# Windowed attention and a gated FFN: one planner for all engines, 32-query units, q and k in 1 KB runs, V as 16 strips, x turned by transfers

## The chip, the cores and the metric

The kernel runs on one core of a Trainium2 chip. The core has a matrix engine (PE, with its weight loads shown as PEld), a vector engine (DVE), a scalar engine (ACT), GpSimd (POOL) and a sync engine (SP), each with its own instruction stream in order; 16 DMA engines move data. POOL and SP issue the transfers here. The metric is device time in microseconds of one execution.

## The reference

Eight batches, eight heads, 512 local and 32 global tokens, head width 64. A global query sees all 544 keys; a local query sees the 32 global keys and the local keys at most 32 positions away. The softmax subtracts the row's maximum. The result, 4352 rows of 512, goes through two products with a gate between.

```python
k_all = concat([k_g, k_l]); v_all = concat([v_g, v_l])
out_g = sm(scale * q_g @ k_all.T) @ v_all
s_ll  = where(abs(pos_q - pos_k) <= 32, scale * q_l @ k_l.T, -1e9)
s_lg  = scale * q_l @ k_g.T
out_l = sm(concat([s_lg, s_ll])) @ concat([v_g, v_l])
x = concat([out_g, out_l]) as (4352, 512)
h = x @ w_in                          # 512 -> 2048
out = (h * clip(h + 3, 0, 6) / 6) @ w_out
```

## The kernel before

All arithmetic on PE is in fp16 with fp32 sums; the loads from POOL's queue convert fp32 to fp16.

**Loads.** `qk_loads` (L98) brings q and k of a batch as four tiles each of 128 tokens, in runs of one head's 64 values (256 bytes in memory). `v_loads` (L110) brings V into `ve`, with the 32 global rows ahead of the local ones, and `shift` (L114, L115) makes `vo`, the same shifted by 64 rows, by two transfers on SP. `load_w_in` and `load_w_out` follow the first batch's loads on POOL.

**Attention.** `pair_qk` (L180, L183) turns two heads of q and of k by eight transposes of 128x128 into one PSUM tile, and ACT copies it to `qk`. A block is (batch, 128 queries `j`, four heads `qd`), so there are eight local blocks a batch and two global ones. `local_scores` (L202) multiplies units of 64 queries with 128 local and 32 global key columns; four 64x64 parts of the array work side by side. Four times DVE adds the mask, scales and takes the maximum (L210) and ACT takes the exponential (L213). `local_turn` (L221, L223) turns the weights by five transposes; DVE first gathers the global columns of the four heads (`exg`, L215). `local_av_global` (L231) multiplies the global columns with a block-diagonal V (`vgb`, L119); `local_av` (L241) adds the local part with `ve` and `vo`; `normalise` (L255, L256) divides. `local_x` (L264, L268) turns x by four transposes and a DVE copy. `global_scores`, `global_turn` and `global_av` (L283 to L310) do the global queries for four even or odd heads at a time.

**FFN.** `first` (L332) makes 128 columns of h for all 512 tokens of a batch (batch 0 in two halves of 256) by four matmuls into one of three PSUM tiles; ACT (L335) and DVE (L336) make the gate. `second` (L346) sums 16 matmuls for 128 tokens, a quarter at a time; DVE copies (L350), SP stores. The global tokens of all batches come last.

**Order.** Only PE's order is written by hand: per block the value product two blocks back, the scores of this block, the turn of the block before, and between them `fill`, which puts in FFN pieces at a share of 0.8 each time. The other engines get theirs from the framework's scheduler. Transfers use eight completion counters on each of POOL's and SP's sides, and a buffer's load waits for its last readers.

## Time and profile before

| | |
|---|---|
| median of three runs | 411.99 us (411.43 to 412.63) |
| span of the profiled execution | 409.9 us |
| granted PE clock | 1.00 |
| packets of the DMA engines, share of POOL's queue | 117874, 58.7% |

The profiled execution's own time is its span and what lies around it; the three runs stand about 2 us above the span. The page gives per engine the busy time, its share and the instruction count; the slices are fortieths of the span in tenths of busy time. In the groups a line reads: line, engine, operation, output and inputs with sizes, count, then busy time, mean nanoseconds of one, and the idle time before them with what ended it. The stage table lists a stretch, its length, PE's busy time and count, the granted clock, the DMA engines' busy share (packets of one engine overlap, so it can pass 1.00), and GB/s. Matmuls overlap, so the time that one costs is the distance to the start of the next.

### The profile page before, as it was taken

The page shows a single profiled execution, that of the slowest core. Times are in us where ns is not written, and L with a number is a line of the kernel's source. Part 1 is how long each engine was busy: PE and PEld are TensorE (multiplying, and loading weights), DVE is VectorE, ACT ScalarE, POOL GpSimd, SP SyncE. Part 2 cuts the span into 40 slices and gives each one's busy share as a digit, 9 for nine tenths or more (in the row PEclk, how much of TensorE's full clock was granted, in tenths as well). Part 3 has the DMA queues.
Part 4 walks back from the last instruction along what each step waited for, and adds up shares of the span by engine and source line. Part 5 has one row for each costly group of instructions (what it writes and reads, how often), then busy time and mean ns, then how long its engine had stood idle before and what let it go on. Part 6 is the DMA issues. An engine that isn't in the chain of part 4 may idle for free.

```text
span 409.9 us, 10488 instructions
## 1 busy us (share of the span) xinstructions
PE 358.8 (88%) x4104; PEld 201.7 (49%) x4104; DVE 265.1 (65%) x1073; ACT 253.3 (62%) x549; POOL 120.0 (29%) x166
## 2 busy tenths in 40 slices
PE   0516388799999999999999999999999999999996
PEld 0404256565545554555445545554555455444642
DVE  2414357885689568865896669756984698558611
ACT  1624368885678658965786668756976586446500
POOL 8925996920920074006500370004000000000000
PEclk9999999999999999999999999999999999999999
DMA  9999999941990199107920493019201100110021
GB/s 90 87 219 200 160 145 126 159 35 53 115 152 3 43 100 137 41 28 91 150 55 27 68 165 60 26 40 92 57 19 36 54 2 2 53 54 0 2 77 77
DMA packets 117874, 31.75 MB, mean 77 GB/s; under 512 B 109888, under 2 KB 111936, under 8 KB 117824
## 3 DMA queue, kind: packets, MB, share of 16 engines
q0 software_dynamic: 111552, 17.84, 58.7%
q1 hardware_dynamic: 6272, 13.24, 9.9%
q8 instruction: 32, 0.52, 0.5%
q14 instruction: 18, 0.15, 0.1%
HBM read 35.65 MB, written 8.91 MB: 109 GB/s over the span
## 4 chain that ended last, share of the span: by engine, by line
PE 58%; DVE 15%; ACT 11%; POOL 7%; DMA 5%; issue 3%; ACTq 0%; POOLq 0%
PE m L346 29%; PE m L332 12%; DVE gt L336 8%; ACT ex L213 6%; DMA win<-in_moe_w_in_dram 4%; ACT t L335 3%; PE t L180 3%; PE t L221 3%; PE a L241 3%; DVE sm L210 3%; PE s L202 3%; ACT et L226 2%; PE a L231 2%; POOL qn L98 2%; POOL kn L98 2%
## 5 line engine op out<-in xcount | busy, mean ns | idle before, releaser
L332 PE MATMUL m<-xt,win 128*128 128x512 f16 (+1 forms) x576 | 122.3, 358 | 7.1 <-DVE gt L336 5.7
L346 PE MATMUL m<-wout,gt 128*128 128x512 f16 x512 | 121.6, 379 | 0.0
L213 ACT ACTIVATE ex<-sm,mx 128x160 f16<-128x160 f32 x256 | 89.0, 418 | 47.2 <-DVE mx L210 47.2
L336 DVE SCALAR_TENSOR_TENSOR gt<-t,m 128x512 f16<-128x512 f32 (+1 forms) x144 | 84.2, 623 | 21.1 <-ACT t L335 20.7
L335 ACT ACTIVATE t<-m 128x512 f32<-128x512 f32 (+1 forms) x160 | 77.2, 527 | 19.9 <-PE m L332 18.8
L332 PEld LDWEIGHTS <-win 128*128 128x128 f16 x640 | 61.1, 98 | 57.1 <-issue 11.7
L210 DVE CUSTOM_DVE_ANT_0 sm<-s,mask 128x160 f32<-128x160 f32 x256 | 67.7, 319 | 10.2 <-PE s L202 10.0
L346 PEld LDWEIGHTS <-gt 128*128 128x128 f16 x512 | 47.3, 98 | 44.6
L226 ACT COPY et<-t 128x640 f16<-128x640 f16 x64 | 43.9, 686 | 29.9 <-PE t L223 29.9
L350 DVE COPY ot<-m 128x512 f32<-128x512 f32 x34 | 23.5, 691 | 36.8 <-PE m L346 36.8
L183 ACT COPY qk<-t 128x1024 f16<-128x1024 f16 x32 | 32.0, 1007 | 16.9 <-PE t L180 16.9
L98 POOL DMA_DIRECT2D qn<-in_q_l_dram x32 | 29.3, 917 | 36.6 <-PE t L180 35.7
L110 POOL DMA_DIRECT2D ve<-in_v_l_dram x40 | 32.3, 861 | 0.0
L98 POOL DMA_DIRECT2D kn<-in_k_l_dram x32 | 29.4, 920 | 0.0
L241 PE MATMUL a<-vo,et 128*64 128x65 f16 x256 | 20.7, 204 | 9.4 <-DMA vo<-ve 9.4
L180 PE MATMUL t<-ident,qn 128*128 128x128 f16 x128 | 14.2, 232 | 16.0 <-POOL ident masks.py:199 9.6
L256 DVE TENSOR_TENSOR x<-a,rec 128x256 f16<-128x256 f32 x64 | 27.0, 422 | 1.4
L110 POOL DMA_DIRECT2D vgn<-in_v_g_dram x8 | 6.0, 752 | 73.1 <-DVE vgb L119 73.1
L231 PE MATMUL a<-vgb,et 128*128 128x264 f16 x64 | 18.3, 285 | 10.1 <-ACT et L226 7.0
L221 PE MATMUL t<-ident,ex 128*128 128x128 f16 x256 | 26.7, 230 | 0.0
L215 DVE COPY exg<-ex 128x128 f16<-128x128 f16 x64 | 15.9, 249 | 15.3 <-ACT ex L213 15.0
L202 PEld LDWEIGHTS <-qk 64*64 64x64 f16 x1024 | 15.9, 111 | 18.4 <-issue 14.1
(68 smaller groups left out, 378.2 us busy)
## 6 DMA issues: line engine op xcount, KB each, us to landing
out_dram<-ot SPq DMA_DIRECT2D x32, 256.0 KB, 2.0
vo<-ve SPq DMA_DIRECT2D x16, 264.0 KB, 3.8
qn<-in_q_l_dram POOLq DMA_DIRECT2D x32, 128.0 KB, 5.0
kn<-in_k_l_dram POOLq DMA_DIRECT2D x32, 128.0 KB, 5.2
ve<-in_v_l_dram POOLq DMA_DIRECT2D x24, 128.0 KB, 5.2
win<-in_moe_w_in_dram POOLq DMA_DIRECT2D x4, 512.0 KB, 11.6
wout<-in_moe_w_out_dram POOLq DMA_DIRECT2D x16, 128.0 KB, 4.9
ve<-in_v_l_dram POOLq DMA_DIRECT2D x8, 96.0 KB, 5.0
```

The costliest lines, as they stand in the source:

```text
L98: return [lambda o=o, i=i: nc.gpsimd.dma_start(out=o, in_=i) for o, i in work]
L110: work = [lambda o=o, i=i: nc.gpsimd.dma_start(out=o, in_=i) for o, i in work]
L183: nc.scalar.copy(out=dst, in_=ps.rearrange("d (i s) -> d i s", i=2))
L210: nc.vector.tensor_tensor_reduce(out=sm, in0=ps[:, e, pi * U:(pi + 1) * U], in1=m, scale=-scale, scalar=3.0e38, op0=ALU.add, op1=ALU.min, ...
L213: nc.scalar.activation(out=ex[:, h, :], in_=sm, func=EXP, scale=-1.0, bias=mx)
L221: nc.tensor.matmul(out=ps[:, h * P:(h + 1) * P], lhsT=ex[:, h, Sg:U], rhs=ident, is_transpose=True)
L226: nc.scalar.copy(out=et, in_=ps)
L241: nc.tensor.matmul(out=ps[s * HW:(s + 1) * HW, h, 0:D + 1], lhsT=et[:, h * P + s * HW:h * P + (s + 1) * HW], rhs=v[:, j, 4 * qd + h, 0:D + 1],
L332: nc.tensor.matmul(out=ps[:, 0:n], lhsT=w_in_t[m][:, c * P:(c + 1) * P], rhs=x[:, m, 0:n], start=(m == 0), stop=(m == NP - 1))
L335: nc.scalar.activation(out=t1[:, 0:n], in_=ps[:, 0:n], func=RELU, bias=0.5, scale=1.0 / 6.0)
L336: nc.vector.scalar_tensor_tensor(out=g[:, 0:n], in0=t1[:, 0:n], scalar=1.0, in1=ps[:, 0:n], op0=ALU.min, op1=ALU.mult)
L346: nc.tensor.matmul(out=ps, lhsT=gs[c][:, t0:t0 + P], rhs=w_out_t[c], start=(c == 0), stop=(c == NDFF - 1))
```

## The change

The kernel is written anew in its attention and its order; the FFN's arithmetic stays.

- Queries go in units of 32: each unit has 96 local key columns and 32 global ones, 128 in all, on 64x32 parts of the array (`scores` in `local`). A step is (batch, 128 queries) with all eight heads, 32 steps in all; the weights of one head are a 128x128 tile and are turned by one transpose each.
- V stands as 16 strips a batch: `vs` holds for each 32-query unit its 96 local and the 32 global rows on 128 partitions, so one matmul a unit and head makes the whole value product (128x32 parts). Strips of batches 0 and 1 are copied by DVE or POOL, 34 copies each; those of the others go by six transfers on SP, and the global rows by four more in every batch.
- q and k are loaded with four successive tokens on one partition, a run of 1 KB; two loads a batch (eight in batch 0). The transposes make 64 rows each, two heads into one tile (128x64 parts), and the copy to `qkT` undoes the order of tokens.
- x is turned by a transposing transfer on SP, 128x512 each (`to_x`), and the global x likewise.
- Every piece of work is an `Op` with a cost and dependencies; `Plan.run` simulates the five engines and the two transfer queues and emits the instructions of all five in the order found. `pick` chooses on PE: full-array attention work first, work on parts of the array when five FFN pieces have passed, when no FFN piece is ready, or when the array is already divided, else FFN. The plan has no term for the completion counters.
- Masks and identity are made ahead of the first load on POOL; w_in is loaded in halves, and batch 1's q and k come between w_in and w_out.
- The global x goes into the FFN's first product per batch column; buffers: three PSUM tiles for the FFN as before, two banks for scores, one tile for turns, two banks for value products.

The core of the diff, the removed parts first:

```diff
-        def shift():
-            nc.sync.dma_start(out=vo[r][0:HW, :, :, :], in_=ve[r][HW:P, 0:NJ, :, :])
-            nc.sync.dma_start(out=vo[r][HW:P, :, :, :], in_=ve[r][0:HW, 1:NJ + 1, :, :])
...
-    def pair_qk(b, p):
-        st = state[b]
-        ps = t_tile(2 * Sl)
-        for i, nat in enumerate((st["qn"], st["kn"])):
-            for j in range(NJ):
-                c0 = i * Sl + j * P
-                nc.tensor.matmul(out=ps[:, c0:c0 + P], lhsT=nat[:, j, p * P:(p + 1) * P],
-                                 rhs=ident, is_transpose=True)
-        dst = qk[b % 2][p].rearrange("d (i c) -> d i c", i=2)[:, :, Sg:Sg + Sl]
-        nc.scalar.copy(out=dst, in_=ps.rearrange("d (i s) -> d i s", i=2))
...
-            for w, (c0, n) in enumerate(((0, Sg), (Sg, P))):
-                for s in range(2):
-                    for e in range(2):
-                        rows = slice(e * D, (e + 1) * D)
-                        lhs = t[rows, Sg + j * P + s * HW:Sg + j * P + (s + 1) * HW]
-                        if w == 0:
-                            rhs = st["gt"][rows, p, gc:gc + Sg]
-                        else:
-                            k0 = KC + (2 * j + s) * HW
-                            rhs = t[rows, k0:k0 + P]
-                        nc.tensor.matmul(out=ps[s * HW:(s + 1) * HW, e, pi * U + c0:pi * U + c0 + n],
-                                         lhsT=lhs, rhs=rhs)
...
-    def local_x(b, j, x):
-        st = state[b]
-        flat = x.rearrange("q h d -> q (h d)")
-        ps = t_tile(NP * P)
-        for p in range(NP):
-            nc.tensor.matmul(out=ps[:, p * P:(p + 1) * P], lhsT=flat[:, p * P:(p + 1) * P], rhs=ident,
-                             is_transpose=True)
-        if j == 0:
-            st["xt"] = xtp.tile([P, NP, Sl], FP16, tag="xt", name="xt")
-        nc.vector.tensor_copy(out=st["xt"][:, :, j * P:(j + 1) * P],
-                              in_=ps.rearrange("d (p q) -> d p q", p=NP))
...
-        share = 0.8
...
+    SWITCH = 95.0
+    LAT = {"PE": 230.0, "ACT": 160.0, "DVE": 120.0, "POOL": 150.0, "SP": 0.0}
...
+        def begin(op, e):
+            nonlocal count
+            cost = op.cost[op.engine.index(e)] if isinstance(op.engine, tuple) else op.cost
+            if e == "PE":
+                if op.mode != self.pe_mode:
+                    cost += self.SWITCH
+                self.pe_mode = op.mode
+            for r in op.take:
+                self.free[r] -= 1
+            op.start, op.on = self.now, e
+            if isinstance(cost, tuple):
+                issue, moved = cost
+                self.busy[e] = self.now + issue
+                drain()
+                queues[e].append([op, moved, self.now + issue])
+                op.done = math.inf
+                look()
+            else:
+                self.busy[e] = self.now + cost
+                self.work[e] += cost
+                op.done = self.now + cost + op.lat
...
+                    can = [op for op in self.ready[e] if able(op)]
+                    if not can:
+                        continue
+                    op = pick(self, can) if e == "PE" else min(can, key=lambda o: (o.rank, o.at))
+                    if op is not None:
+                        begin(op, e)
+                        moved = True
...
+    def dma(rows, run, issue=None):
+        return (300 + 0.56 * rows if issue is None else issue, rows * (22.6 + run / 27.0) / 16)
+    def moved(rows, run):
+        return (420.0, rows * (22.6 + run / 27.0) / 16)
+    DMA_LAT = 1500.0
...
+    def act(n, ptr=False):
+        return (186.0 if ptr else 50.0) + n / 1.2
+    def dve(n, fast=1):
+        return 65.0 + n / 0.96 / fast
...
+    def loads(b):
+        r = b % 2
+        k = 0
+        prev = [turned[b - 2][p] if b >= 2 else None for p in range(NP)]
+        if b == 0:
+            for p in range(NP):
+                for i, (t, src) in enumerate(((qn, q_l), (kn, k_l))):
+                    hs = slice(2 * p, 2 * p + 2)
+                    nat[b][i][p] = load(t[r][:, hs, :], src[b, hs].rearrange("h (p r) d -> p h (r d)", r=R),
+                                        2 * P, 1024, [], (b, 0, p, i), f"{'qk'[i]}n{b}.{p}")
+        else:
+            for i, (t, src) in enumerate(((qn, q_l), (kn, k_l))):
+                o = load(t[r], src[b].rearrange("h (p r) d -> p h (r d)", r=R), H * P, 1024, prev, (b, 0, i) if b > 1 else (0, 4, 2, i),
+                         f"{'qk'[i]}n{b}")
+                for p in range(NP):
+                    nat[b][i][p] = o
...
+        vdep = [strips[b - 2][i] for i in range(len(strips[b - 2]))] + [av_op[b - 2][NJ]] if b >= 2 else [z[r]]
+        ops = [load(vn[r][0:Sg, NJ, :, 0:D], v_g[b].rearrange("h s d -> s h d"), H * Sg, 256, vdep, (b, 2, 0),
+                    f"vg{b}")]
+        for i in range(NJ):
+            ops.append(load(vn[r][:, i, :, 0:D], v_l[b, :, i * P:(i + 1) * P, :].rearrange("h s d -> s h d"),
+                            H * P, 256, vdep, (b, 2, i + 1), f"vn{b}.{i}"))
+        vload[b] = ops
+        parts = [
+            (flat[W:P], nf[0:Sg, NJ:NJ + 1, :].unsqueeze(2), Sg * NU, [ops[0]], True),
+            (flat[0:W, :, 1, :], nf[0:W, 0:NJ, :], W * NJ, ops[1:], False),
+            (flat[0:W, :, 2, :], nf[Sg:P, 0:NJ, :], W * NJ, ops[1:], False),
+            (flat[0:2 * Sg, :, 3, :], nf[2 * Sg:P, 0:NJ, :], 2 * Sg * NJ, ops[1:], False),
+            (flat[2 * Sg:W, 0:NJ - 1, 3, :], nf[0:Sg, 1:NJ, :], Sg * (NJ - 1), ops[1:], False),
+            (flat[0:Sg, 1:NJ, 0, :], nf[3 * Sg:P, 0:NJ - 1, :], Sg * (NJ - 1), ops[1:], False),
+            (flat[Sg:W, :, 0, :], nf[0:2 * Sg, 0:NJ, :], 2 * Sg * NJ, ops[1:], False),
+        ]
+        free = [av_op[b - 2][j] for j in range(NJ)] if b >= 2 else [z[r]]
+        strips[b] = []
+        if b in MOVED:
+            quads = ((1, 0, W, 0, 0), (2, 0, Sg, Sg, 0), (2, Sg, Sg, 2 * Sg, 0), (2, 2 * Sg, Sg, W, 0),
+                     (3, 0, 2 * Sg, 2 * Sg, 0), (0, Sg, Sg, 0, 0), (0, 2 * Sg, Sg, Sg, 0), (0, 0, Sg, W, -1),
+                     (3, 2 * Sg, Sg, 0, 1))
+            for j in range(NJ):
+                for u, d0, rows, s0, d in quads:
+                    if not 0 <= j + d < NJ:
+                        continue
+                    n = H * D1
+                    o = add(("DVE", "POOL"), (dve(n, 2), 200 + n), None, [ops[j + 1 + d]] + free, (b, 1, j, 9),
+                            lat=150.0, what=f"move{b}.{j}")
+                    def emit(o=o, j=j, u=u, d0=d0, rows=rows, s0=s0, d=d):
+                        eng = nc.vector if o.on == "DVE" else nc.gpsimd
+                        eng.tensor_copy(out=flat[d0:d0 + rows, j, u, :], in_=nf[s0:s0 + rows, j + d, :])
+                    o.emit = emit
+                    strip_j[b][j].append(o)
+                    strips[b].append(o)
+            parts = parts[:1]
...
+    def turn_qk(b, p):
+        r = b % 2
+        def emit():
+            for i, t in enumerate((qn[r], kn[r])):
+                for a in range(R):
+                    c0 = i * Sl + a * P
+                    for e in range(2):
+                        nc.tensor.matmul(out=pst[e * D:(e + 1) * D, c0:c0 + P],
+                                         lhsT=t[:, 2 * p + e, a * D:(a + 1) * D], rhs=ident, is_transpose=True)
+        deps = [nat[b][0][p], nat[b][1][p], idop]
+        dst = qkT[r][p]
+        free = [s_op[b - 2][j] for j in range(NJ + 2)] if b >= 2 else [z[r]]
+        pe = add("PE", 450.0, emit, deps + free, (b, 0, p), mode="128x64", take=("t",), what=f"T{b}.{p}")
+        def emit_copy(i):
+            c0 = i * (Sl + Sg)
+            d = dst[:, c0:c0 + Sl].rearrange("d (p r) -> d r p", r=R)
+            s = pst[:, i * Sl:(i + 1) * Sl].rearrange("d (r p) -> d r p", r=R)
+            return d, s
+        halves = []
+        for i in range(2):
+            halves.append(copy(lambda i=i: emit_copy(i)[0], lambda i=i: emit_copy(i)[1], Sl,
+                               [pe] + halves, (b, 0, p, i), give=("t",) if i else (), what=f"Tc{b}.{p}"))
+        turned[b][p] = halves[1]
...
+    def local(b, j):
+        r, n = b % 2, step[0]
+        step[0] += 1
+        gt = gT[(b // 2) % 2]
+        gc = (b % 2) * 2 * Sg + Sg
+        def scores():
+            for p in range(NP):
+                t = qkT[r][p]
+                for w in range(2):
+                    for u in range(UJ):
+                        c = j * P + u * Sg
+                        for e in range(2):
+                            rows = slice(e * D, (e + 1) * D)
+                            o = pss[u * Sg:(u + 1) * Sg, e, p * P:(p + 1) * P]
+                            if w == 0:
+                                nc.tensor.matmul(out=o[:, 0:W], lhsT=t[rows, c:c + Sg],
+                                                 rhs=t[rows, Sl + c:Sl + c + W])
+                            else:
+                                nc.tensor.matmul(out=o[:, W:P], lhsT=t[rows, c:c + Sg], rhs=gt[rows, p, gc:gc + Sg])
...
+        def turn():
+            for h in range(H):
+                nc.tensor.matmul(out=pst[:, h * P:(h + 1) * P], lhsT=ex[ie][:, h, :], rhs=ident, is_transpose=True)
+        k = n % NET
+        tn = add("PE", 8 * 56.0, turn, exps + [et_use.get(k)], (b, 1, j), take=("t",), what=f"E{b}.{j}")
+        ex_use[ie] = tn
+        tc_ = copy(lambda: et[k], lambda: pst, H * P, [tn], (b, 1, j, 9), fast=2, give=("t",),
+                   what=f"Ec{b}.{j}")
+        def av():
+            for h in range(H):
+                for u in range(UJ):
+                    q = slice(u * Sg, (u + 1) * Sg)
+                    c0 = (h % 4) * D1
+                    nc.tensor.matmul(out=psa[q, h // 4, c0:c0 + D + 1],
+                                     lhsT=et[k][:, h * P + u * Sg:h * P + (u + 1) * Sg],
+                                     rhs=vs[r][:, j * UJ + u, h, 0:D + 1])
+        a = add("PE", 8 * 32.0, av, [tc_] + strip_j[b][j], (b, 1, j), mode="128x32", take=("a",), what=f"A{b}.{j}")
+        et_use[k] = a
+        av_op[b][j] = a
+        ix = n % 3
+        def norm():
+            acc = psa[:, :, 0:4 * D1].rearrange("q c (h d) -> q c h d", d=D1)
+            rr = rec[ix].rearrange("q (c h) -> q c h", c=2).unsqueeze(3)
+            nc.vector.reciprocal(out=rr, in_=acc[:, :, :, D:D + 1])
+            nc.vector.tensor_tensor(out=xs[ix].rearrange("q (c h d) -> q c h d", c=2, d=D), in0=acc[:, :, :, 0:D],
+                                    in1=rr.to_broadcast([P, 2, 4, D]), op=ALU.mult)
+        nm = add("DVE", 120 + dve(H * D), norm, [a, x_use.get(ix)], (b, 1, j, 10), give=("a",), what=f"norm{b}.{j}")
+        def to_x():
+            nc.sync.dma_start_transpose(out=xt[b % 3][:, :, j * P:(j + 1) * P], in_=xs[ix])
+        free = m1_done[b - 3] if b >= 3 else []
+        xo = add("SP", (900.0, 1100.0), to_x, [nm] + free, (b, 1, j, 11), DMA_LAT, what=f"X{b}.{j}")
+        x_use[ix] = xo
+        x_op[b][j] = xo
...
+    state = {"since": 0}
+    PACE = 5
+    def pick(plan, can):
+        att = [o for o in can if o.what[0] in "TEGSA"]
+        ffn = [o for o in can if o.what[0] == "M"]
+        full = [o for o in att if o.mode == "full"]
+        if full:
+            return min(full, key=lambda o: (o.rank, o.at))
+        tiled = [o for o in att if o.mode != "full"]
+        if tiled and (not ffn or state["since"] >= PACE or plan.pe_mode != "full"):
+            same = [o for o in tiled if o.mode == plan.pe_mode]
+            order = {"128x64": 0, "64x32": 1, "128x32": 2}
+            o = min(same or tiled, key=lambda o: (order[o.mode], o.rank, o.at))
+            if plan.pe_mode == "full":
+                state["since"] = 0
+            return o
+        if ffn:
+            m2 = [o for o in ffn if o.what.startswith("M2")]
+            m1 = [o for o in ffn if o.what == "M1"]
+            cont = [o for o in m2 if o.what == "M2+"]
+            backlog = sum(o.cost if not isinstance(o.cost, tuple) else o.cost[0] for o in plan.ready["ACT"])
+            if m1 and (backlog < 1500 or not m2):
+                o = min(m1, key=lambda o: (o.rank, o.at))
+            elif cont:
+                o = min(cont, key=lambda o: (o.rank, o.at))
+            else:
+                o = min(m2, key=lambda o: (o.rank, o.at))
+            state["since"] += 1
+            return o
+        return None
+    order = plan.run(pick)
+    E = mybir.EngineType
+    with tc.manual_schedule(engines={E.PE, E.Activation, E.DVE, E.Pool, E.SP}):
+        for op in order:
+            op.emit()
```

## The prediction

> **What bounds the kernel now.** I read the page first (share of each engine, the slices, the costliest groups), then busy time by stage, then the order of time on PE inside one step, then the waits of POOL's queue and the DMA packets of single stretches.
>
> ```profile
> span 409.9 us, 10488 instructions
> PE 358.8 (88%) x4104; PEld 201.7 (49%) x4104; DVE 265.1 (65%) x1073; ACT 253.3 (62%) x549; POOL 120.0 (29%) x166
> PE   0516388799999999999999999999999999999996
> DMA  9999999941990199107920493019201100110021
> L346 PE MATMUL m<-wout,gt 128*128 128x512 f16 x512 | 121.6, 379 | 0.0
> q0 software_dynamic: 111552, 17.84, 58.7%
> ```
>
> PE is full from about slice 9 on, the DMA engines fill the first eight slices (82 us) and then not half of each. The stages, busy microseconds of PE:
>
> ```profile
> 0.00:40.00 40.00, 13.18 (x169) 1.00 1.25 148
> 40.00:60.00 20.00, 12.15 (x151) 1.00 1.85 155
> 194.10:236.50 42.40, 41.37 (x495) 1.00 0.72 77
> 321.50:364.00 42.50, 40.85 (x473) 1.00 0.08 32
> ```
>
> A batch repeats every 42.5 us. What PE does in it is read from starts, not from durations, which overlap. The reader takes the distance from one group to the next:
>
> ```profile
> 199.53 0.28 PE L231 MATMUL a<-vgb,et 128*128 128x264 f16 x1
> 199.73 0.21 PE L202 MATMUL s<-gt,qk 64*64 64x32 f16 x4
> ...
> 200.03 0.22 PE L241 MATMUL a<-ve,et 128*64 128x65 f16 x1
> ...
> 200.28 0.40 PE L221 MATMUL t<-ident,ex 128*128 128x128 f16 x4
> 200.51 0.22 PE L223 MATMUL t<-ident,exg 128*128 128x128 f16 x1
> 200.57 0.38 PE L332 MATMUL m<-xt,win 128*128 128x512 f16 x1
> ...
> 318.19 0.33 PE L310 MATMUL a<-ve,et 128*32 128x65 f16 x20
> 318.46 0.45 PE L298 MATMUL t<-ident,eg 128*128 128x128 f16 x5
> ```
>
> One block of attention takes 0.20+0.30+0.25+0.29 = 1.04 us. Twelve 512-column matmuls take 2.59 us in the chain (0.216 us each, 2.37 columns a ns), so the columns of the block are 0.11+0.14+0.11+0.27 = 0.63 us (small tiles run side by side) and its three changes of array shape 0.41 us, 0.137 us each. A batch of before is then 128 FFN matmuls x 0.216 = 27.6, 8 blocks 8.3, 48 transposes x 0.056 = 2.7, two global blocks about 2.2: 40.9 us, and 1.6 us of stalls. With the global FFN (64 x 0.109 + 32 x 0.216 = 13.9) PE has 8 x 40.9 + 13.9 = 341 us of work in 410; 69 us are lost: 55 before 109 us (by then it has done 54 us of work: batch 0 and the attention of batch 1), about 9 in stalls, 5 at the end.
>
> **The change on PE.** By count of the new order: FFN unchanged: 992 matmuls of 512 columns x 0.216 = 214 and 192 of 256 x 0.109 = 21, 235 us. The q/k transposes, 512 into half the array, run two abreast: 256 x 0.056 = 14. 336 + 16 full transposes: 20 (before 101 a batch; the x transposes and the fifth transpose of each block are gone). Local scores: 64 matmuls of 96 and 32 columns on 8 tiles, 4 x 128 columns = 0.216 us x 32 = 7; global scores 16 x 0.23 = 4; local attention-value 8 x 65 columns = 0.22 x 32 = 7; global 0.27 x 8 = 2. Changes of shape: 183 instead of 240, x 0.137 = 25. Sum 314 us: 27 less than before, 37.5 a batch.
>
> **Other engines.** DVE a batch: 32 maxima at 0.245-0.033 = 0.21 (7), gates 16 x 0.63 (10), normalisation 4 x 0.9 (4), global maxima 2; the exg, vgb and xt copies (2.0+1.0+1.7) are gone. ACT: 32 exponentials at a step of 0.29 (9), relus 8, global 1.4. The shared copies (q/k, exponentials, out) are about 11 of ACT time, so both stand near 27 of 39 us. They hide beside PE; if the steps of the softmax chain slip, PE waits (a rival below).
>
> **DMA.** From 4 to 18 us only 128-byte packets run: 156.4% x 14 us x 16 / 11120 = 31.5 ns each; from 34 to 43 us the 1024-byte ones come to 98. q and k now go as 512-byte packets; no row has them, the bounds are 31.5 and 98, I take 60 by size. A batch: 2048 x 60 / 16 = 7.7 us of q, k (before 16), v and g 4864 x 31.5 / 16 = 9.6, the strips 1984 pieces of 1056 bytes at about 60 (bounds 32 and 98: 4 to 12 us) 7.4 where vo had 2, stores 3. Transposing transfers: no row. 131 KB as 64 packets of 2 KB at 95 ns (out, from the last 29 us) would be 0.4 us, as 2048 pieces of 64 bytes at 31.5 ns 4.0; I take whole rows of 256 bytes, 512 x 31.5 / 16 = 1.0 us, since that is what a 128-column block reads. 4.3 a batch. Sum 32 of 39 us: close, but under PE. The Trainium skill (DMA: Bandwidth & Descriptors, Latency and other measured facts) gives 261 GB/s for a transposing DMA: an estimate of 0.5 us each by that page, and 30 us a batch; no run here shows it.
>
> **The start, on the path.** POOL stands still when too many loads are out:
>
> ```profile
> POOL wout L129 <- DMA win<-in_moe_w_in_dram: 9.9, 4, 3.4
> 29.14 0.53 POOL L129 DMA_DIRECT2D wout<-in_moe_w_out_dram  x1 [3.41 <-DMA win<-in_moe_w_in_dram]
> ```
>
> In the changed kernel every load waits for the one eight before it, and the planner's costs do not count that. POOL carries 17 of the 34 strip copies of batch 0, and 15 of batch 1, behind such loads. Following the queue: q, k land by 12.5 us (7.7 from 3.5), g and v by 23.5, the first half of w_in (1024 packets of 2 KB, by size 172 ns, 11 us for all) by 29. wout 1 waits for that, so the first POOL strip copies start at 29.5; no row has them, the 128-element select of POOL takes 0.29 us, a copy of 528 between 0.29 and 4 x 0.29: I take 0.75. With three more waits 17 copies end near 44 (before: two DMA shifts held PE until 31). PE has the last value matmul of batch 0 ahead of the first FFN group, so FFN starts at 45, not 53; its first product comes in 32 groups of four 256-column matmuls, and three such groups take 1.52 us at the end of before (379.87, 381.39, 382.92 in the chain): 16 us, then 13.8 of the second product and 7 of transposes and scores: 82 us. Batch 1's POOL copies stand behind the loads of batches 2 and 3: the last of these waits until half of v of batch 2 has landed, that is 66 (w_in by 34, batch 1's q, k 7.7, wout 2048 x 98 / 16 = 12.5, v 8.7, about 3 of SP's transfers) + 7.7 + 2 + 4.6 + about 3 more = 83. Then 15 x 0.75 = 11, value matmul, norm, transfer (1 + 2 to land): batch 1's FFN at 98. Had they not stood there, the chain of two softmax steps (max 1.7, exp, turn, copy 0.9, value, norm 0.9, each in DVE's order) from 82 would still give 94. By 98 PE has done 37.5 + 9.9 = 47: 51 lost, against 55.
>
> **Sum.** 98 + (314 - 47) + 5 where batches 2 and 3 run dry of FFN work between value matmul and transfer + 8 of stalls as before + 5 at the end = 383 us of span. The profiled span of 409.9 stands 2.1 under the median of 411.99, so 385. No change can be told within about 0.3% (411.43 to 412.63 for the same kernel).
>
> **Rivals.**
> - *Start clear.* POOL copies cost 0.3 us or the loads wait less: FFN at 34 and batch 1 at 84, all else equal: 371. For it: a select takes 0.29. Against: the waits of 3.4 us above.
> - *Transfers become the bound* (slower). Place: SP's queue, where 10 strip transfers, 5 transposes and 4 stores a batch stand in one order; in before SP stood 121.7 us for v's loads ahead of vo, and no x was behind it. It decides from about 3.5 us each: loads, strips and stores take 27.7 a batch, six batches after 98 us must take 43 us, not 38.8, to undo the 25 gained, so 4.25 transfers (four and the small global one) get 15 us. At 4.0, the upper bound: 6 x (27.7 + 17 - 38.8) = +35: 420. For it: no row excludes it. Against: 256-byte rows.
> - *PE cannot be fed* (slower). A step's scores are 64 pairs of weight load and matmul in a row; the longest tight run of before is 41 pairs (317.89 to 318.75). If pairs past 41 go at the 0.058 us of a transpose, a step gains 23 x 0.058 = 1.3 us, 24 steps after the start: +32, 417. Against: 20 pairs in 0.27 us, change of shape included.
>   The Trainium skill (TensorE: Matmul & The Clock Gate, the section Wait — 56ns, not 53.3ns?) has a floor of about 25 ns from start to start: 64 x 25 = 1.6 us by it, about the same loss. The row above, 13.5 ns a pair, disagrees with it for 20 pairs; no run here shows 64.
> - *The written order slips.* All five engines now follow one planned order; where a real time is longer than planned (gate 0.63, planned 0.60; the eight-load wait, not planned), PE stands behind a matmul that waits, with FFN work behind it. Stalls of 1.6 a batch becoming 6: 6 x 4.4 = +26, 411. For it: PE waits on DVE gt and ACT et in before as well. Against: both engines have 12 us spare a batch.
>
> **How the numbers follow.** Start as reckoned 0.52 (own range 372 to 398: POOL copies, prices of 1056-byte pieces, stalls 0 to 3 a batch); start clear 0.20; transfers 0.10; feeding 0.06; slipped order 0.12. Faster is the first two, and half of the slipped order and a fifth of the transfers: 0.80; within 0.3% 0.03; slower 0.17. To leave out 2 in 10: 358 (start clear and no stalls) to 417.
>
> **What would show it.** PE's group distances: 64 score pairs in about 0.35 us with the change of shape, or over 1 us. A batch in about 39 us between the same points, and FFN matmuls still 0.216 apart. FFN's first group near 45 us, batch 1's near 98, with POOL copies of strips waiting behind loads just before. DMA busy near 0.8 in the middle batches, the transposing transfers landing in 2 to 4 us; at over 5, or with SP's queue waiting for its own transfers, the prediction is wrong. It is also wrong if PE's waits in mid-batches exceed 3 us a batch, whoever ends them.

## The result, and the profile after

The changed kernel takes 427.89 us (median of four runs, 427.05 to 428.73), the kernel before on the same chip 412.31. The ratio is 1.0365 (95% interval 1.0331 to 1.0398): slower, where 385 had been forecast. Ratios, here and below, compare mean times and leave out the three executions (one each of pace2, three and three_stepped_write) that ran over 1.5% above the fastest of their kernel, while the medians include them. The profiled execution has a span of 426.5 us. From the page of the changed kernel (share of each engine; the 40 slices of PE, of its granted clock and of the DMA engines; the first DMA queue; the groups of the matmuls' gate and of the q/k copy):

```profile
span 426.5 us, 13518 instructions
PE 349.1 (82%) x5632; PEld 196.7 (46%) x5632; DVE 233.8 (55%) x884; ACT 280.6 (66%) x553; POOL 94.8 (22%) x144
PE   2244698965999765999659999999899999999995
PEclk9999989985899955999957999999999999999999
DMA  7999999641999234975990599539612120201112
q0 software_dynamic: 60000, 17.57, 43.1%
L660 DVE SCALAR_TENSOR_TENSOR gl<-t,m 128x512 f16<-128x512 f32 (+1 forms) x160 | 95.0, 606 | 62.3 <-ACT t L656 61.0
L290 ACT COPY qkT<-t 128x512 f16<-128x512 f16 x57 | 70.1, 1346 | 24.4 <-PE t L450 22.0
```

PE's busy time fell, from 358.8 to 349.1 us, so matmul work was saved as intended. But PE is idle for 426.5 - 349.1 = 77.4 us, where before it was 409.9 - 358.8 = 51.1. PE's row has three dips beyond the start (slices 9 and 10, 14 to 16, 20 and 21), and the clock row dips with them, a slice late. (Both kernels' first slices read 9 in the clock row, but no record of the clock stands behind these; see the last section.) By stage (busy us of PE, PEld, DVE, ACT and POOL with their instructions; granted clock; DMA share; GB/s):

```profile
54.00:107.40 53.40, 41.90 (x755) 26.90 (x756) 33.17 (x124) 33.52 (x72) 22.09 (x33) 0.82 0.92 106
107.40:146.00 38.60, 36.38 (x492) 18.12 (x488) 17.84 (x65) 27.48 (x49) 8.16 (x11) 0.98 0.85 123
146.00:184.00 38.00, 27.22 (x620) 17.33 (x606) 22.17 (x99) 29.70 (x62) 5.84 (x7) 0.73 0.75 119
184.00:226.00 42.00, 32.02 (x703) 19.63 (x704) 24.11 (x107) 30.64 (x62) 5.84 (x7) 0.83 0.89 144
270.00:320.00 50.00, 45.70 (x760) 24.48 (x758) 34.40 (x113) 43.69 (x83) 4.09 (x5) 1.00 0.71 113
```

The dips are stretches in which no FFN matmul starts: 19.0 us from 88.4, 23.1 from 144.8 and 18.4 from 208.1 (distances between successive FFN matmuls in the trace). One batch's FFN is used up there, and the next batch's x is not ready. PE still does the attention that is ready: it is idle for 9.1, 10.8 and 8.9 us of the three. What it waits for is in the chain of the second dip (start, duration, engine, tile, line):

```profile
148.76 1.30 ACT qkT L290
...
150.10 1.03 PE t L528 x8
...
151.96 1.08 PE t L450 x16
...
153.06 2.44 ACT qkT L290 x2
...
155.55 1.02 PE t L528 x8
...
160.10 2.43 ACT qkT L290 x2
...
165.21 2.45 ACT qkT L290 x2
```

From 142 to 168 us 33.2% of the chain is ACT's q/k copies and 4.7% DVE's. In the planned order a pair of q/k transposes of batch 3 (L450) stands between the steps of batch 2's softmax. Each pair fills the one turn tile `t`, and the two copies that empty it take 2.45 us, for which the exponentials' transposes (L528) and global transposes stand behind it. At the lower clock those transposes take 1.0 us in place of 0.45. Over the whole execution PE waits for ACT's q/k copies for 22.9 us, longer than for any other work (what waited and for what; us in all, times, longest):

```profile
PE t L450 <- ACT qkT L290: 8.2, 4, 2.5
PE t L528 <- ACT qkT L290: 5.9, 5, 1.9
PE t L474 <- ACT qkT L290: 3.9, 3, 2.5
PE t L603 <- ACT qkT L290: 2.5, 1, 2.5
PE s L501 <- ACT qkT L290: 2.4, 2, 1.3
```

The copy itself is the plainest difference from before. There, the same transposes were copied 1024 values at a time, straight; the group is

```profile
L183 ACT COPY qk<-t 128x1024 f16<-128x1024 f16 x32 | 32.0, 1007 | 16.9 <-PE t L180 16.9
```

that is 1.0 us a head pair. Now a pair is two copies of 512 values of 1.35 us, and each writes its values four apart (8 bytes), to undo the token order that the 1 KB runs bring.

### The profile page after: what moved, and what is told of

It reads as the page before. It is cut to its first block, busy times and chain, and to the rows that moved or that the text cites. A ratio compares the mean times of both kernels' runs of the same rounds, so it can differ in the third digit from the quotient of the medians.

```text
span 426.5 us, 13518 instructions
## 1 busy us (share of the span) xinstructions
PE 349.1 (82%) x5632; PEld 196.7 (46%) x5632; DVE 233.8 (55%) x884; ACT 280.6 (66%) x553; POOL 94.8 (22%) x144
## 4 chain that ended last, share of the span: by engine, by line
PE 60%; DVE 13%; ACT 12%; POOL 5%; DMA 5%; issue 4%; ACTq 0%; DVEq 0%; POOLq 0%
PE m L675 25%; PE m L650 21%; ACT qkT L290 7%; DVE sm L515 4%; PE t L528 3%; ACT t L656 3%; PE t L450 3%; DMA win<-in_moe_w_in_dram 3%; DVE gl L660 2%; DMA xt<-x 2%; PE s L501 2%; PE a L540 2%; DVE vs L410 2%; DVE qkT L292 2%; PE t L603 1%
## 5 line engine op out<-in xcount | busy, mean ns | idle before, releaser
L660 DVE SCALAR_TENSOR_TENSOR gl<-t,m 128x512 f16<-128x512 f32 (+1 forms) x160 | 95.0, 606 | 62.3 <-ACT t L656 61.0
L675 PE MATMUL m<-wout,gl 128*128 128x512 f16 x544 | 126.2, 379 | 1.7 <-DVE gl L660 1.7
L519 ACT ACTIVATE ex<-sm,mx 128x128 f16<-128x128 f32 x256 | 82.9, 394 | 26.8 <-DVE mx L515 26.4
L515 DVE CUSTOM_DVE_ANT_0 sm<-s,mask 128x128 f32<-128x128 f32 x256 | 58.9, 287 | 50.7 <-PE s L504 50.4
L290 ACT COPY qkT<-t 128x512 f16<-128x512 f16 x57 | 70.1, 1346 | 24.4 <-PE t L450 22.0
L675 PEld LDWEIGHTS <-gl 128*128 128x128 f16 x544 | 51.2, 98 | 59.2 <-issue 2.3
L290 ACT COPY et<-t 128x1024 f16<-128x1024 f16 (+1 forms) x34 | 29.9, 880 | 21.5 <-PE t L528 12.9
L501 PE MATMUL s<-qkT 64*32 64x96 f16 x1024 | 21.9, 220 | 13.8 <-DVE mx L515 11.4
L272 POOL DMA_DIRECT2D vn<-in_v_g_dram x8 | 4.7, 588 | 128.0 <-PE a L617 92.5
L450 PE MATMUL t<-ident,qn 128*64 128x128 f16 x256 | 15.3, 248 | 19.1 <-ACT qkT L290 8.2
L272 POOL DMA_DIRECT2D vn<-in_v_l_dram x32 | 28.1, 889 | 6.5 <-DVE gl L660 4.7
L528 PE MATMUL t<-ident,ex 128*128 128x128 f16 x256 | 24.2, 250 | 5.9 <-ACT qkT L290 5.9
L501 PEld LDWEIGHTS <-qkT 64*32 64x32 f16 x1024 | 16.8, 95 | 22.6 <-issue 20.4
L528 PEld LDWEIGHTS <-ex 128*128 128x128 f16 x256 | 19.5, 113 | 11.5 <-issue 6.6
L450 PEld LDWEIGHTS <-qn 128*64 128x64 f16 x256 | 10.7, 122 | 29.0 <-issue 21.8
L552 DVE TENSOR_TENSOR x<-a,rec 128x512 f16<-128x512 f32 x32 | 22.1, 691 | 1.1
```

Source lines behind the costliest of these rows:

```text
L272: return add("POOL", dma(rows, run), lambda: nc.gpsimd.dma_start(out=dst, in_=src), deps, rank, DMA_LAT, what=what)
L290: nc.scalar.copy(out=dst(), in_=src())
L450: nc.tensor.matmul(out=pst[e * D:(e + 1) * D, c0:c0 + P], lhsT=t[:, 2 * p + e, a * D:(a + 1) * D], rhs=ident, is_transpose=True)
L501: nc.tensor.matmul(out=o[:, 0:W], lhsT=t[rows, c:c + Sg], rhs=t[rows, Sl + c:Sl + c + W])
L515: nc.vector.tensor_tensor_reduce(out=sm[i3][h], in0=pss[:, e, p * P:(p + 1) * P], in1=m, scale=-scale, scalar=3.0e38, op0=ALU.add, op1=ALU ...
L519: nc.scalar.activation(out=ex[ie][:, h, :], in_=sm[i3][h], func=EXP, scale=-1.0, bias=mx[i3][h])
```

## The experiments

Theories at the outset: the stepped copy holds the softmax chain by its own price; the order does the damage, being planned for a price that the copy doesn't have; the strip copies of batches 0 and 1 hold the start, and everything after it. Later two more: the pacing of attention pieces runs the batches dry; the hold of the turn tile is what a dear copy costs.

Each kernel is compared with the kernel before, measured beside it on the same chip (its medians there were 412.3 to 413.0). The third and fourth columns are from the profiled execution.

| kernel | median us | PE busy / idle | clock | first products of batches 0, 1, 2, 3 begin |
|---|---|---|---|---|
| changed | 427.9 | 349.1 / 77.4 | 0.932 | 44.4, 107.4, 167.9, 226.5 |
| no_reorder | 408.7 | 348.7 / 59.2 | 0.934 | 43.5, 103.6, 157.2, 214.4 |
| strided_read | 408.9 | 347.6 / 59.0 | 0.934 | 43.2, 103.0, 156.7, 213.1 |
| true_price | 405.9 | 341.9 / 63.3 | 0.955 | 45.0, 105.0, 153.0, 207.1 |
| strips_by_transfer | 428.5 | 346.1 / 83.0 | 0.952 | 53.0, 118.2, 167.1, 227.1 |
| dve_strips | 406.0 | 345.0 / 60.4 | 0.940 | 39.8, 101.6, 153.5, 200.8 |
| pace2 | 407.3 | 342.6 / 58.1 | 0.963 | 43.7, 103.4, 152.7, 187.4 |
| two_no_prices | 399.7 | 342.5 / 55.5 | 0.964 | 37.7, 98.7, 148.4, 183.8 |
| three | 394.0 | 340.2 / 51.4 | 0.972 | 38.9, 101.2, 149.0, 184.4 |
| three_stepped_write | 407.7 | 339.7 / 62.3 | 0.970 | 40.7, 107.7, 158.2, 192.6 |
| halves | 392.9 | 338.3 / 49.7 | 0.989 | 38.7, 88.7, 139.8, 177.8 |
| side_by_side | 424.4 | 346.9 / 76.3 | 0.939 | 45.0, 106.2, 164.3, 222.8 |
| halves_side | 404.9 | 345.8 / 56.5 | 0.969 | 40.2, 92.7, 147.2, 181.0 |

### What the copy's steps cost: no_reorder and strided_read

no_reorder copies straight on both sides. It leaves out the undoing of the token order, and all else, the planned order too, is as in the changed kernel.

```diff
-            d = dst[:, c0:c0 + Sl].rearrange("d (p r) -> d r p", r=R)
-            s = pst[:, i * Sl:(i + 1) * Sl].rearrange("d (r p) -> d r p", r=R)
+            d = dst[:, c0:c0 + Sl]
+            s = pst[:, i * Sl:(i + 1) * Sl]
```

> The copies from the turn tile to qkT go straight, 512 values in a row on both sides, in the same planned order; the tokens then stand in another order, so this leaves out the undoing of the order of tokens. Theory A (the copies that write every fourth value, 1.31 us instead of the 0.5 to 0.6 of other 512-value copies, hold the one turn tile and make the dry stretches of batches 2 and 3): the copy falls to 0.55-0.65 us, the span to 380-395 us, the stretch from batch 2's first FFN product to batch 3's falls from 59 us to under 48. Theory B (the start and the planned order, not the copies): the copy gets faster but the span stays above 415 us. Theory C (PE runs at a lowered clock because of its gaps, whatever makes them): follows A, clock above 0.97.

strided_read undoes the order, with the step on the other side: it writes contiguously and reads PSUM 128 values apart.

```diff
-            d = dst[:, c0:c0 + Sl].rearrange("d (p r) -> d r p", r=R)
-            s = pst[:, i * Sl:(i + 1) * Sl].rearrange("d (r p) -> d r p", r=R)
+            d = dst[:, c0:c0 + Sl].rearrange("d (p r) -> d p r", r=R)
+            s = pst[:, i * Sl:(i + 1) * Sl].rearrange("d (r p) -> d p r", r=R)
```

> The same copies with the same result, but written in a row and read with a step of 128 values from PSUM. If the step on the written side is what costs, the copy takes 0.55-0.7 us and the span is that of the straight copy within 3 us. If any step costs, the copy stays at 1.2-1.3 us and the span at 424-430 us.

no_reorder: 408.68 (ratio 0.9902, 0.9873 to 0.9932). strided_read: 408.86 (0.9919, 0.9889 to 0.9949). The group of the copy in strided_read (min/median/max ns):

```profile
L290 ACT COPY qkT<-t x57: 575/587/592, 6.8 to 307.5; 128x512 f16<-128x512 f16 x57
L292 DVE COPY qkT<-t x7: 683/691/692, 65.4 to 288.8; 128x512 f16<-128x512 f16 x7
```

On ACT, 1.31 us (median) becomes 0.587, the same as straight (0.586). On DVE 1.30 becomes 0.69 (0.425 straight). So it is the stepped write into SBUF that costs, and the same reordering done by a stepped read is free on ACT. With nothing else changed that alone is worth 19 us and turns the kernel from slower to slightly faster than before (0.8%). PE's waits for ACT's q/k copies fall by 17.6 us, from 22.9 to 5.3, which is nearly the whole gain.

The copy itself came out as theory A of no_reorder said, but the span did not: 407.9 us lies between A's 380 to 395 and B's over 415. The three stretches without FFN stay, at 19.0, 17.3 and 17.5 us (19.0, 17.7 and 17.5 in strided_read), and from batch 2's first product to batch 3's it is 57.2 us, where A wanted under 48. The clock stays at 0.934, where C wanted over 0.97. So the copy's price by itself does not make the stretches.

### The plan for the wrong price: true_price

The copies stay at 1.3 us; the planner, which had priced them as `act(512)` = 0.477 us and `dve(512)` = 0.598, is told 1.23, and plans all orders anew. (The edit adds a line, so the kernel's later lines stand one lower: L291 is L290 of the others.)

```diff
-            op = add(("ACT", "DVE"), (act(n), dve(n, fast)), None, deps, rank, lat=150.0, give=give, what=what)
+            cost = (1230.0, 1230.0) if what.startswith("Tc") else (act(n), dve(n, fast))
+            op = add(("ACT", "DVE"), cost, None, deps, rank, lat=150.0, give=give, what=what)
```

> The copies stay as they are, but the planner counts 1.23 us for each instead of 0.48 or 0.60, and plans anew. Theory A with the price as the damage (engine time and the held tile): at most 10 us better, 415-427. Theory D (the damage is that the written order was planned for another price): 390-405, dry stretches gone with the copies still at 1.3 us.

405.88 (0.9835, 0.9797 to 0.9872), just over the 390 to 405 of theory D and well under the 415 of A. The stretches without FFN are shorter, 13.2, 8.4 and 14.8 us, but not gone as D had it. The copies are no cheaper, but the planner now spreads them over two engines:

```profile
L291 ACT COPY qkT<-t 128x512 f16<-128x512 f16 x39 | 49.4, 1319 | 22.3 <-PE t L451 19.6
L293 DVE COPY qkT<-t 128x512 f16<-128x512 f16 x25 | 32.5, 1301 | 7.5 <-ACT qkT L291 5.3
```

and 22 us are gone. Price and plan are not two shares of the loss that add up: a cheap copy in the old order, or the dear copy in an order that knows of it, each brings the kernel to 406 to 409.

### The start: strips_by_transfer

The strips of batches 0 and 1 go by SP's transfers too, so that no copy stands on POOL or DVE (`MOVED = ()` in place of `(0, 1)`).

> Strips of batches 0 and 1 go by transfers on SP as those of the others, no strip copies on POOL or DVE, planned anew. Theory B (start): the first FFN product comes at 38-46 us, batch 1's before 100 instead of 107.4, span 412-421. Theory A: the start gains at most 7 us and the dry stretches stay: 418-428.

428.51 (1.0398, 1.0359 to 1.0437): not to be told from the changed kernel. Neither theory had the start come later, but it did, the first FFN group at 53.0 us in place of 44.4, batch 1's at 118.2 in place of 107.4. For the start the copies, late as they were, are the better way; this run doesn't tell whether POOL is their right place.

### The rest: strip copies on DVE, the pacing, the prices

From here the copies write in order, as in strided_read. One more thing is visible in its order. This is its chain before the second dip:

```profile
126.47 0.16 PE s L501 x6
...
127.08 3.56 PE m L675 x16
130.64 0.45 PE t L528 x8
131.09 0.86 PE m L675 x4
131.95 0.16 PE s L501 x6
...
137.43 0.16 PE s L501 x6
```

The scores of batch 2 (L501) come every 5.5 us, with just 20 FFN matmuls, five pieces of four, between them: that is `PACE = 5` in `pick`, which lets a tiled piece in only after five FFN pieces. The FFN of the batch in front holds 27.6 us of matmuls and ends at 139 us; by then only the third of four blocks has its scores.

dve_strips puts all 68 strip copies on DVE:

```diff
-                    o = add(("DVE", "POOL"), (dve(n, 2), 200 + n), None, [ops[j + 1 + d]] + free, (b, 1, j, 9),
+                    o = add("DVE", dve(n, 2), None, [ops[j + 1 + d]] + free, (b, 1, j, 9),
```

> The q/k copies write in order (as in strided_read, 408.9 us), and the 68 strip copies of batches 0 and 1 all stand on DVE, none on POOL, so no copy waits behind a load in POOL's queue and none runs beside a POOL copy (DVE took 0.29 us a copy alone, 0.60 to 0.67 beside POOL). Theory 'POOL copies hold the start': first FFN group near 34 us (43 in strided_read), batch 1's near 93 (103), the total near 398. Theory 'the paced softmax chain holds batch 1, whatever copies the strips': first FFN earlier by some us, batch 1's at 100 or later, the total 405 to 409.

pace2 has `PACE = 2`.

> The q/k copies write in order, and the planner lets an attention piece of tiled shape in after 2 FFN pieces in place of 5 (each piece four matmuls, 0.86 us). Theory 'the pacing runs batches 2 and 3 dry': ten such pieces a batch at 4.3 us and more each are 43 us, while a batch holds 28 us of FFN, so attention is not ready when FFN is used up; with 2 the stretch without FFN before batch 3 (17.5 us at 196 in strided_read) is gone or under 5, the one before batch 2 is shorter, the total 388 to 396, in spite of more changes of array shape. Theory 'late loads and real prices make the dry stretches': stretches of 15 us and more stay, the total 404 to 412.

three has both, and the planner's prices of copies as measured:

```diff
-            op = add(("ACT", "DVE"), (act(n), dve(n, fast)), None, deps, rank, lat=150.0, give=give, what=what)
+            op = add(("ACT", "DVE"), (586.0, 690.0) if what.startswith("Tc") else (act(n) + 75, dve(n, fast) + 75), None, deps, rank, lat=150.0, give=give, what=what)
```

> Both of these, and the planner told measured prices of its copies (q/k copies 0.586 us on ACT and 0.690 on DVE, 75 ns more on the others). If start and pacing add up: first FFN near 34, batch 1's near 92, no stretch without FFN over 10 us after 130, the total 375 to 388, faster than before. If the start is held by something else: 388 to 400.

two_no_prices is three without that last edit.

> As three, but the planner keeps its own prices of the copies. The copies write in order, so real and planned price differ by 0.1 us only. If start and pacing make the gain of three, 392 to 397; if the told prices make it, 400 to 406.

Measured: dve_strips 406.01 (0.9846, 0.9792 to 0.9901), pace2 407.30 (0.9869, 0.9844 to 0.9895), two_no_prices 399.70 (0.9680, 0.9630 to 0.9729), three 394.03 (0.9518, 0.9464 to 0.9572). Against strided_read's 408.9 the two edits bring 2.9 and 1.6 us alone, and 9.2 together; the told prices 5.7 more. The larger gains that the expectations held out did not come: dve_strips, three and two_no_prices ended at or just beside their second, smaller ranges, and pace2 in a range for which its expectation had a different reason. (The profiled execution of pace2 is its fastest, 402.5 us.)

dve_strips brought the first FFN group forward by 3.4 us and batch 1's by 1.4 only, so POOL's queue was not by itself what held batch 1. (The work of the copies is still there, on DVE, and the order is planned anew, so this does not show what did.) The expectation of pace2 failed in an instructive way. The stretch before batch 3 vanished as expected, and batch 3's first product began 26 us earlier (187.4 against 213.1). But from there to the global FFN it took 183 us, against 163 in strided_read. Busy time of both in that part (strided_read first; a fence for each):

```profile
213.00:376.00 163.00, 163.00 (x2396) 83.87 (x2389) 102.19 (x338) 109.22 (x231) 9.95 (x12) 0.99 0.53 89
```

```profile
187.00:370.00 183.00, 176.05 (x2784) 91.01 (x2781) 115.29 (x415) 117.12 (x261) 11.87 (x15) 0.99 0.54 103
```

pace2 issues 2784 matmuls there, strided_read 2396: the attention of later batches, which strided_read had done in its dry stretches, is still to do. Of the 20 us more, 13 are PE's busy time and 7 its idle time. A stretch without FFN is not lost time one for one. As these rows read, its loss is what PE waits inside it and what the lower clock there costs; no run separates the two.

In three, both are down: PE is idle for 51.4 us, and the middle of its rows is nearly full.

```profile
PE   2442869895999975999999999999999999999995
PEclk9999989987799998999999999999999999999999
```

### The dear copy under the better plan: three_stepped_write

As three, with the stepped write, and 1.23 us told for it.

> As three, but the q/k copies write stepped as in the changed kernel (1.3 us each) and the planner is told so. If the price alone is on the path wherever a pair stands between transposes (32 pairs x 1.4 us more = 45 us at most, 19 measured in the changed kernel's order): 405 to 414. If the plan can hide the copies once it knows them: within 6 us of three, 394 to 400.

407.68 (0.9839, 0.9779 to 0.9900), 13.7 us over three, in the range of the first of its two cases. Even a plan that knows them does not hide these copies; they are 8% of the chain that ended last (ACT 6, DVE 2):

```profile
PE m L675 30%; PE m L650 24%; ACT qkT L290 6%; PE t L450 4%; DMA xt<-x 4%; DVE gl L660 3%; PE t L528 3%; PE s L501 3%; DVE sm L515 2%; DVE qkT L292 2%; PE a L540 2%; ACT t L656 1%; PE s L504 1%; PE t L603 1%; DVE x L552 1%
```

### x by halves: halves

As three, and the first products of batches 1 and 2 in two halves of 256 columns.

```diff
-        parts = ((0, 2), (2, 4)) if b == 0 else ((0, 4),)
+        parts = ((0, 2), (2, 4)) if b < 3 else ((0, 4),)
```

> As three (394.0 us), and the first product of batches 1 and 2 comes in two halves of 256 columns as that of batch 0 does, so that it can begin when two of the four query blocks have their x. If the wait for the whole of x is what leaves PE without FFN work before batches 1 and 2 (11.5 and 6.9 us, the last groups at a lower granted clock): those stretches fall below 6 us and the total to 382 to 390. If the softmax chain of the two last blocks is the bound all the same, or 32 more relus and 32 more gates (0.3 to 0.4 us each, ACT and DVE) cost as much: 392 to 400.

392.94 (0.9530, 0.9479 to 0.9582), not to be told from three. The stretches without FFN fell as expected (4.9 us at most after 60 us), batch 1's first product began 12.5 us earlier, the clock rose to 0.989, and still the time is the same to within the intervals: PE's idle time in the profiled executions fell by 1.7 us and its busy time by 1.9. So the total lies in the second range, and the wait for the whole of x was not what it hung on. What had filled those stretches, attention of the coming batch, moved behind, as in pace2.

### Two copies at once: side_by_side and halves_side

Here the second copy of a pair no longer waits, in the plan, for the first.

```diff
-                               [pe] + halves, (b, 0, p, i), give=("t",) if i else (), what=f"Tc{b}.{p}"))
+                               [pe], (b, 0, p, i), give=("t",) if i else (), what=f"Tc{b}.{p}"))
```

> As true_price (405.9 us: stepped writes of 1.3 us, and the planner knows it), but the second copy of a pair no longer waits for the first, so ACT and DVE can make them at the same time and the one turn tile is held for about 1.35 us in place of 2.45. If the hold of that tile in the softmax chain is what a dear copy costs: 395 to 401. If it is the work of the copies on ACT and DVE, which stays: 403 to 408.

> As halves (392.9 us; copies written in order, 0.59 on ACT and 0.69 on DVE), with the two copies of a pair side by side. The hold falls from about 1.25 to 0.7 us: 388 to 392 if it is still on the path between transposes, 392 to 396 if the order around it decides.

side_by_side: 424.40 (1.0287, 1.0243 to 1.0332), 18.5 us over true_price. halves_side: 404.86 (0.9818, 0.9784 to 0.9851), 11.9 over halves, each above both of its ranges. The copies did not run at the same time. From the timeline of side_by_side (start, us, engine, line; in brackets the wait):

```profile
147.27 1.30 ACT L291 COPY qkT<-t 128x512 f16<-128x512 f16 x1
...
148.60 1.29 DVE L293 COPY qkT<-t 128x512 f16<-128x512 f16 x1 [1.25 <-ACT qkT L291]
```

In 31 of 32 pairs one began 31 to 35 ns after the other's end: the built program still makes the later one wait for the first (the bracket). In halves_side, too, most pairs followed each other with 31 to 35 ns between. So the plan was wrong in a new way. It put the second copy at the head of DVE's queue 1.3 us too early, and DVE stood there with the maxima and gates behind it, 49.5 us in all:

```profile
L293 DVE COPY qkT<-t 128x512 f16<-128x512 f16 x32 | 41.5, 1298 | 52.1 <-ACT qkT L291 49.5
```

Whether a shorter hold of the turn tile would help was therefore not tested and stays open. What the runs do show is the price of an order planned for what the machine doesn't do: 18.5 us with dear copies, 11.9 with cheap ones.

## Why the prediction was wrong

**The step that failed: "The shared copies (q/k, exponentials, out) are about 11 of ACT time ... They hide beside PE".** The term of the q/k copies was mis-sized. At the planner's price they are 64 x 0.48 / 8 = 3.8 us a batch, and before they took 32 x 1.007 / 8 = 4.0. Measured, they kept ACT busy for 70.1 us and DVE for 9.1, together 9.9 a batch. The diff shows the stepped pattern (`"d (p r) -> d r p"` as the destination), and the prediction counted the copy without looking at it. The Trainium skill (Vector Engine (DVE) Microarchitecture Reference, section Measured stream behaviour on trn2) says that a port keeps its rate only for runs of at least two adjacent 4-byte words, and gives 2.50 to 2.51 ns a column for a destination that steps 24 such words at every element (1.71 where it hops 4 KiB). The trace is near the first figure on DVE: 1.30 us / 512 = 2.54 ns, though its values are of 2 bytes and 8 bytes apart. It shows the same on ACT, for which that section gives no figure.

**"They hide beside PE" failed by its argument too.** It compared sums of busy time, 27 of 39 us a batch. ACT was busy for only 66% of the span, and still its q/k copies led PE's waits (22.9 us, and 5.3 when they were cheap), since they hold the one turn tile inside the softmax chain. The sum of an engine says nothing of a resource that one of its instructions holds.

**"5 where batches 2 and 3 run dry".** The stretches without FFN are 23.1 and 18.4 us there, and PE is idle for 10.8 + 8.9 = 20 us of them. From batch 1's first product to the end it took 426.5 - 107.4 = 319 us, where 285 had been forecast: 34 of the 43 us of the error. PE is busy for 285 of the 319 and idle for 34, where the sum had 267 of work and 18 of losses; so about half of the error is idle time, and half is work that took longer than reckoned. The cheap copy took 19 us off the whole, the pacing, the strips on DVE and the told prices 15 more. In three this part takes 391.6 - 101.2 = 290 us, 5 over the forecast.

**The start.** The first FFN group: 44.4 us, forecast 45, in part by luck, since POOL's copies of batch 0 ended at 41.3 and not near 44, and 3 us passed after them in place of 1. Batch 0's FFN ended at 88.4, not 82. POOL's copies of batch 1, behind the loads: forecast "from 83, 11 us", in the changed kernel's timeline

```profile
79.09 0.89 POOL L272 DMA_DIRECT2D kn<-in_k_l_dram  x1
80.02 10.79 POOL L410 COPY vs<-vn 96x528 f16<-96x528 f16 x16
```

at 0.62 us each, where 0.75 was taken. But batch 1's FFN came at 107.4, not 98, and with the POOL copies gone (dve_strips) still at 101.6 against strided_read's 103.0. So the queue was read rightly, but it was not by itself what the end hung on. The last POOL copy ends at 90.8, and 16.6 us more pass. The prediction had two softmax steps left from 82 us on, which gave 94. In the trace all four of batch 1 were still to do: their maxima on DVE begin at 81.5, 87.6, 92.5 and 96.5 us (from 81 to 107 us DVE's strip copies are 20.9% of the chain and its maxima 18.3%). 9 us of the error are here.

**PE's work.** By the distance to the next group: 8 exponential transposes 0.45 us at full clock (forecast 0.45), 32 value matmuls 0.37 (0.36), 16 q/k transposes 0.57 (0.59), FFN matmuls 0.216 apart (0.216). The 64 score pairs take 0.61, not 0.35: 32 x 0.26 = 8 us more than the term had, the largest of these differences. What sets the 0.61 no run shows. The rival that PE cannot be fed had 1.3 us more a step, not 0.26; in that size it fell. At 9.5 ns a pair the trace disagrees with the floor of about 25 ns from start to start that the Trainium skill gives (TensorE: Matmul & The Clock Gate, section Wait — 56ns, not 53.3ns?). The saving on PE was there: 358.8 us of busy time before, 338.3 in halves. In the changed kernel half of these 20 us are missing (349.1). Its lower clock is the likely reason: after the start, 36 us of PE's busy time lie in stretches with a granted clock of 0.50, against 7 us in halves, and work at half the clock takes about twice as long (the transposes above: 1.0 us for 0.45).

**DMA.** 512-byte packets 60 ns (median; forecast 60), 1056-byte pieces 60 (60). A transposing transfer is 512 packets of 256 bytes at 18 ns (median; mean 23), 0.58 us of all engines (0.74 by the mean), where 1.0 was taken. The 0.5 that the prediction estimated from the Trainium skill (DMA: Bandwidth & Descriptors, section Latency and other measured facts) is below both. The transfer lands in 2.4 us by the median, as expected:

```profile
xt<-x SPq DMA_TRANSPOSE x32, 2.4
```

The rival of the transfers fell with that.

**The rivals.** "The written order slips" was the right kind: real times longer than planned, PE behind a matmul that waits. It named the gate (planned 0.60, now 0.606) and the loads, and gave 411. The instruction that slipped most was the copy (planned 0.48, real 1.35). The sentence "Against: both engines have 12 us spare a batch" was the argument that let it stand at 0.12. Of the tests that the prediction set itself, PE waits of over 3 us in mid-batch was the one that came true (10.8 us idle from 146 to 184 us).

**What the two errors leave.** With the copy's step on the other side and the plan mended, three reaches 394.0, and halves 392.9, 4.8% and 4.7% under the kernel before and 8% under the changed one. Of the 9 us by which three stays over 385, 3 lie ahead of batch 1's first product and 5 behind it; the score pairs' 8 us are of that size, but no run separates them. That the lower clock comes from the idle stretches is read from their coincidence in the rows, and was not tested by itself.

## What to carry to other kernels

Look at the innermost step of every copy that is added or re-shaped: a 2-byte write 8 bytes apart cost more than twice the straight one here, and the same reordering on the reading side cost ACT nothing (DVE 0.27 us a copy). Where one planner writes the order of all engines, check each of its prices against a row of the profile, for here an operation priced too low held up other engines through the tile that it held, though its own engine was idle a third of the time. And a stretch in which the main work pauses is not worth its length: whatever other work it held has to be done elsewhere when it is closed (pace2 began batch 3's first product 26 us earlier than strided_read and, even in its fastest execution, ended only 6 us earlier).

## What was not expected of the hardware

- A copy of 512 fp16 values from PSUM: written straight 0.586 us on ACT and 0.425 on DVE; read 128 values apart 0.587 and 0.69; written 4 values apart 1.31 and 1.30.
- The granted clock fell to 0.73 over 146 to 184 us, with PE busy 72% of that stretch, and 8 transposes took 1.03 us in place of 0.45. The trace's records show it in steps: 0.50 from 91.9 to 109.0, 150.0 to 170.5 and 211.4 to 228.5 us, each beginning 3.3 to 5.2 us after the last FFN matmul and ending 1.6 to 2.6 us after the next one began (and once for 3.4 us, from 54.4).
- A clock of 1.00 in the first slices is no measurement. The first record stands at 55.7 us before and at 47.6 us in the changed kernel, and up to there both ran PE at half speed: transposes of 128 columns began 0.107 us apart and first-product matmuls of 256 columns 0.213, later 0.056 and 0.109 (medians). So part of the 55 us that the prediction counts as lost before 109 us is slow work and not waiting. In six of the 28 other executions of the kernel before, the mean clock reads 0.95, and they took no longer (411.6 to 413.2 us) than the rest (411.1 to 414.6): a low mean alone says nothing of the time.
- DVE's strip copies of 528 values took 0.29 us by the median, but six of the seven that began while POOL's copies of batch 1 ran (80.0 to 90.8 us) took 0.60 to 0.67. With none on POOL the longest of 68 took 0.356 in three:

```profile
L410 DVE COPY vs<-vn x68: 282/289/356, 19.1 to 96.3; 32x528 f16<-32x528 f16 x52, 96x528 f16<-96x528 f16 x8, 64x528 f16<-64x528 f16 x8
```

- Two copies in a row on one engine overlap: two of 1.35 us took 2.45. Across two engines, where the second waits for the first, it began 31 to 35 ns after the first ended (side_by_side).
